# A kernel's head and tail: unit matrix and masks made on VectorE, GpSimd's first 64-bit addition put first, the last unit's halves interleaved

## The chip, the core and the metric

The kernel runs on one core of a Trainium2 chip. The time is device microseconds of one execution; the span is the time from the first to the last instruction of the profiled execution. The engines are called by their names in the profile: PE (TensorE), DVE (VectorE), ACT (ScalarE), POOL (GpSimd) and SP (SyncE, which issues DMAs).

## What is computed

Two attention blocks, A and B, each on its own x (2048 x 512), with 32 heads of 16 columns, and their outputs side by side in a 2048 x 1024 result, all in bfloat16:

```
qkv = (x @ wqkv) split into q, k, v, heads of 16
A (linear attention):  pq, pk = phi(q), phi(k);  phi(t) = t + 1 if t > 0 else exp(t), plus 1e-6
                       o = (pq @ (pk^T v)) / (pq . sum(pk) + 1e-6);  out = o @ wo
B (softmax attention): p = softmax(q k^T / 4);  o = p v;  out = o @ wo
```

## The kernel before

Block B is nearly all of the work. Its 32 heads are walked in 32 units: four groups of eight heads, in each four stretches of 512 queries, and in each of these an even and an odd half (four heads each, one per quarter of the PE array). A unit has 64 score blocks: 16 key tiles of 128 for each of the four heads. PE computes a block of scores (128 keys x 512 queries, line 916). Its exponential is taken in one of two ways. ACT does two or three blocks in one instruction (L1128), or DVE makes a 16-bit integer of the scores that, read as a 16-bit float, is nearly the exponential (L1032); POOL then makes two more copies of such a pair of blocks by adding a constant to four such integers at once, as one 64-bit addition (L1212, two additions for a group of two blocks). PE multiplies the results by the values (L1286) and gathers a unit's sums in one PSUM tile, pPV, in whose 32-row quarters 16 rows are sums and the 17th is the denominator. DVE transposes this tile in blocks of 32 x 32, takes reciprocals of the denominators, scales, and transposes back (L1315 to L1328; for the last unit L1378 to L1383, in two halves of 256 columns, so that the output product of the first half can begin before the second half is done). Block A's work (L623, L738 and others) fills gaps.

The order on each engine is fixed when the program is built. A planner holds a modelled clock for each engine and picks at each step among scores for ACT, scores for DVE, products with the values and small jobs. Its parameters change every 12 modelled us; they stand in the table SEG, one row per stretch. The 24th number of a row, DE3, says from which point on the last unit's groups no longer go to POOL: `late = left[NU - 1] < DE3 and ...`, with `left` the blocks of the last unit not yet taken. Where `late` holds, DVE makes the two copies itself (L1183). Jobs of the tail are put into lists (`urgent`, `urgent2`), each a sequence of steps with an engine and a modelled duration; the planner takes the first job of `urgent` as soon as it can start, and a job's next step when the one before is done.

Instructions wait for each other by semaphores. An instruction on an engine's queue that depends on an earlier one of the same queue also waits for it.

The head, before the planner begins, is written by hand:

- SP and ACT issue the loads: tiles 2 and 3 of x (ON), the first weights (Wb) by ACT; x transposed (xTb), the other weights and A's data by SP.
- DVE clears ZW, ZR and the tile pPV. POOL writes the iota FLG (one element, overwritten later by the flag that says whether scores are too large for this method), the unit matrix identb (`mk_ident`: clear, then select), the mask ZMk (`band`: which 16 rows belong to which of eight heads), clears EA and the start of DI, runs one 64-bit addition on zeros, and then writes the unit matrix identf, the mask BMk and the ones of VNa.
- DVE then reduces ZMk to PAR (even and odd heads' rows, L525), writes the ones of VV (L529, L531) and clears the second half of KM (L533).
- PE runs 30 products on ZW to warm up (L1401), transposes tiles 2 and 3 of x with identb (L1412), runs 8 more warming products, and makes the first keys and queries (L1424). DVE copies the one transposed tile (L609), ACT the other; DVE writes the masked keys KM with PAR (L1434). Then the first scores can be made (L916).

At the end every engine reads the flag (L1664) and jumps over a general softmax, which is in the program but not executed here (L1666), to two last instructions that the block's end adds (L372): a drain and a wait for all engines.

Of the kernel before, what the change touches and what calls it, by code (L numbers as in the profile page):

```python
# [8 lines left out]
F32 = mybir.dt.float32  # L9
# [3 lines left out]
ALU = mybir.AluOpType  # L13
# [225 lines left out]
def bass_concat_heads__linear_attn_block__softmax_full_mha__prompt_kernel(nc, A_x, A_wqkv, A_wo, B_x, B_wqkv, B_wo, out):  # L239
# [132 lines left out]
    with es:  # L372
# [44 lines left out]
        ZMk = sb("ZMk", [128, 8], F32)  # L417
        PAR = sb("PAR", [128, 2], F32)
# [82 lines left out]
        sch.add("pool", lambda e: e.iota(FLG.bitcast(mybir.dt.int32)[0:1, 0:1], [[0, 1]], base=0, channel_multiplier=0), writes=["FLG"])  # L501
        mk_ident(identb, "identb")
# [17 lines left out]
        band(ZMk, 8, 1, "ZMk")  # L520
        sch.add("pool", lambda e: e.memset(EA[:, 512:528], 0.0), writes=["EA"])
        sch.add("pool", lambda e: e.memset(DI[:, 0:64], 0.0), writes=[("DI", 0, 0, 0)])
        sch.add("pool", lambda e: e.int64_add(DW[:, 0:8], DW[:, 8:16], 0), reads=[("DI", 0, 0, 0)], writes=[("DI", 0, 0, 0)])
# [845 lines left out]
        def last_unit(u, t_):  # L1369

            Gp, c, e_ = unit(u)
            k, xb = 4 * Gp + c, (u // 2) % 2
            for h in range(2):
                cs = slice(256 * h, 256 * h + 256)
                o = PVb[:, cs].rearrange("p (m a r) -> p m a r", a=2, r=32)
                xn = XN[:, xb, cs].rearrange("p (m r a) -> p m a r", r=32, a=2)
                zr = ZR[:, 0, 8 * h:8 * h + 8].rearrange("p (m a) -> p m a", a=2)
                st = [("dve", 0.36, f_op("dve", lambda e, cs=cs: e.transpose(PVb[:, cs], PVb[:, cs]), [("PV", g) for g in range(4)], [("PVh", h)])),  # L1378
                      ("dve", 0.12, f_op("dve", lambda e, zr=zr, o=o: e.reciprocal(zr, o[:, :, :, 16]), [("PVh", h)], [("ZRh", h)] + [("ZR", 0)] * (h == 0))),
                      ("dve", 0.2, f_op("dve", lambda e, xn=xn, o=o, zr=zr: e.tensor_tensor(  # L1380
                          xn[:, :, :, 16 * e_:16 * e_ + 16], o[:, :, :, 0:16], zr.unsqueeze(3).broadcast_to([128, 4, 2, 16]), op=ALU.mult),
                          [("PVh", h), ("ZRh", h)], [("XNh", h)] + [("XN", xb, e_)] * (h == 0))),
                      ("dve", 0.2, f_op("dve", lambda e, cs=cs: e.transpose(on_at(k)[:, cs].bitcast(U32), XN[:, xb, cs].bitcast(U32)), [("XN", xb, 0), ("XNh", h)],  # L1383
                                        [("onh", h)] + (on_keys(k) if h == 0 else [])))]
                urgent.append(Job(st, [("zrh", 0)] if h else [("ot", u - 1)], [(1, ("zrh", h)), (3, ("onh", h))], bank=False, ready=t_, prio=-1))
                for tl in (2 * h, 2 * h + 1):
                    lane = "dve" if tl in (1, 3) else "act"
                    def last(bk, tl=tl):
                        tail_mm(tail["bk"][tl], tl, (3,))
                    def fin(bk, tl=tl, lane=lane):  # L1390
                        bk = tail["bk"][tl]
                        sch.add(lane, lambda e: copy_to(lane, lambda: obf(tl), lambda b: f32v(bk))(e, None), reads=[bk[3]], writes=kst(tl))
                        stores.append(sch.add(sch.new_dma_lane(), lambda e: e.dma_start(out[0][(12 + tl) * 128:(13 + tl) * 128, 512:1024], obf(tl)),
                                              reads=kst(tl), queue="act" if tl == 2 else "sp", force_signal=True))
                    urgent2.append(Job([("pe", 0.216, last), (lane, 0.6 if lane == "dve" else 0.52, fin)], [("onh", h), ("tail", tl)], [], bank=False))
# [324 lines left out]
```

## Time and profile before

| | us |
|---|---|
| runs | 657.56, 659.1, 660.05 (median 659.1) |
| profiled execution | 661.47 |
| its span | 660.0 |
| PE, ACT, DVE, POOL busy | 637.7, 632.5, 608.2, 430.0 |
| mean granted clock of PE | 0.994 |

The lines of a timeline read: start, length, engine, line of the kernel, operation, output <- input, shape, count, and in brackets the idle time before it with what ended it. "issue" there means that the engine waited for nothing that the profile shows. In waits, the columns are total, count and longest. Rows with a q behind the engine's name are of its instruction queue (branches, drains, semaphores, DMA issues), which don't count as busy. The line numbers are those of the kernel before.

### The profile page before, as it was taken

What the parts mean: (1) busy time and instruction counts of PE and PEld (TensorE: products, weight loads), DVE (VectorE), ACT (ScalarE), POOL (GpSimd) and SP (SyncE); (2) the same over time, 40 slices, a digit from 0 to 9 for tenths busy, and PEclk for the clock granted to TensorE, in tenths of its full rate; (3) what the DMA queues carried; (4) which work ended last, traced back from release to release, by engine and by line L of the source; (5) the groups of instructions that cost most, each with busy time, mean ns of one, the idle gap of its engine ahead of it and who ended that gap; (6) DMA issues with size and microseconds to landing.
All of it is one profiled execution on the core that took longest, in us unless ns stands there. A gap on an engine that the chain in (4) does not pass through costs nothing.

```text
span 660.0 us, 19615 instructions
## 1 busy us (share of the span) xinstructions
PE 637.7 (97%) x8365; PEld 215.1 (33%) x8366; DVE 608.2 (92%) x1078; ACT 632.5 (96%) x688; POOL 430.0 (65%) x733
## 2 busy tenths in 40 slices
PE   5999999999999999999999999999999999999994
PEld 4434333334333433333333232323222232232221
DVE  3799999999999998999999999999999999988983
ACT  1999999999999999999999999999999999999993
POOL 0367776777876766677767667666777766656550
PEclk9999999999999999999999999999899999999998
DMA  9700010011001000102121111002100001101111
GB/s 218 166 2 2 10 34 13 7 40 20 19 2 33 2 10 5 39 8 44 34 66 33 33 26 27 17 9 51 41 9 18 1 18 42 33 10 35 53 46 44
DMA packets 53229, 21.77 MB, mean 33 GB/s; under 512 B 44176, under 2 KB 52624, under 8 KB 53136
## 3 DMA queue, kind: packets, MB, share of 16 engines
q1 hardware_dynamic: 51664, 19.80, 13.0%
q8 instruction: 67, 1.10, 0.7%
q10 hardware_dynamic: 1472, 0.66, 0.4%
q14 instruction: 26, 0.21, 0.1%
HBM read 4.46 MB, written 4.19 MB: 13 GB/s over the span
## 4 chain that ended last, share of the span: by engine, by line
PE 49%; ACT 40%; DVE 8%; issue 2%; DMA 1%; POOL 0%; DVEq 0%; POOLq 0%
ACT PT L1128 38%; PE pPV L1286 18%; PE pS L916 17%; PE pD L623 6%; DVE DI L1032 4%; PE pS L623 3%; PE pD L722 1%; ACT EA L738 1%; PE pD L916 1%; PE pS L722 1%; DMA KNa<-VNa 1%; DVE pPV L1315 1%; PE pS L679 1%; DVE KNa L609 0%; DVE VNa L828 0%
## 5 line engine op out<-in xcount | busy, mean ns | idle before, releaser
L1128 ACT ACTIVATE PT<-pS 128x1024 f16<-128x1024 f32 (+1 forms) x650 | 619.4, 1102 | 6.6 <-PE pS L916 5.4
L1212 POOL INT64_ADD DI<-DI x714 | 427.0, 611 | 197.5 <-DVE DI L1032 195.4
L1032 DVE TENSOR_SCALAR DI<-pD 128x512 int16<-128x512 f32 x499 | 329.4, 683 | 19.0 <-PE pD L916 14.2
L916 PE MATMUL pS<-QT,KM 32*128 32x512 bf16 x1547 | 263.3, 386 | 3.4 <-ACT PT L1128 2.6
L1286 PE MATMUL pPV<-PT,VV 128*17 128x512 f16 x1333 | 236.3, 381 | 0.0
L1286 PE MATMUL pPV<-DI,VV 128*17 128x512 f16 x1430 | 228.2, 381 | 0.0
L916 PE MATMUL pD<-QT,KM 32*128 32x512 bf16 x501 | 175.5, 385 | 0.4 <-DVE VNa L828 0.2
L1286 PE MATMUL pPV<-DI,VX 128*17 128x512 f16 x715 | 163.9, 382 | 0.3 <-DVE OT L1320 0.2
L1032 DVE TENSOR_SCALAR DI<-pS 128x512 int16<-128x512 f32 x214 | 145.3, 679 | 1.6 <-PE pS L916 1.4
L916 PEld LDWEIGHTS pS<-QT,KM 32*128 32x128 bf16 x1547 | 66.9, 91 | 238.0 <-ACT PT L1128 188.3
L1286 PEld LDWEIGHTS pPV<-PT,VV 128*17 128x17 bf16 x1333 | 52.3, 88 | 45.3 <-issue 36.8
L1286 PEld LDWEIGHTS pPV<-DI,VV 128*17 128x17 bf16 x1430 | 51.6, 88 | 42.7 <-issue 27.8
L916 PEld LDWEIGHTS pD<-QT,KM 32*128 32x128 bf16 x501 | 42.0, 91 | 4.0 <-DVE DI L1032 1.5
L1286 PEld LDWEIGHTS pPV<-DI,VX 128*17 128x17 bf16 x715 | 36.3, 89 | 21.3 <-issue 14.2
L623 PE MATMUL pD<-Wa,xTa 128*32 128x256 bf16 x704 | 28.6, 275 | 0.4 <-DVE DI L1032 0.4
L623 PE MATMUL pD<-xTb,Wb 128*32 128x512 bf16 x336 | 27.8, 396 | 0.0
L1315 DVE STREAM_TRANSPOSE pPV<-pPV 128x512 f32<-128x512 f32 x31 | 22.4, 722 | 0.0
L623 PEld LDWEIGHTS pD<-Wa,xTa 128*32 128x32 bf16 x704 | 14.9, 95 | 10.9 <-issue 6.6
L623 PE MATMUL pD<-xTa,Wa 128*32 128x512 bf16 x192 | 15.7, 384 | 0.3 <-DVE DI L1032 0.2
L738 ACT ACTIVATE EA<-pD 128x512 bf16<-128x512 f32 x24 | 15.8, 657 | 0.0
L623 PE MATMUL pD<-Wa,KNa 128*32 128x512 bf16 x176 | 14.8, 406 | 0.9 <-DMA KNa<-VNa 0.7
L1320 DVE TENSOR_TENSOR OT<-pPV,ZR 128x256 bf16<-128x256 f32 x31 | 13.9, 447 | 1.1
(137 smaller groups left out, 343.4 us busy)
## 6 DMA issues: line engine op xcount, KB each, us to landing
out_dram<-KNa SPq DMA_DIRECT2D x31, 128.0 KB, 1.7
Wa<-in_A_wqkv_dram SPq DMA_DIRECT2D x1, 1536.0 KB, 8.4
KM<-KR SPq DMA_DIRECT2D x96, 16.0 KB, 1.8
Wb<-in_B_wqkv_dram SPq DMA_DIRECT2D x2, 384.0 KB, 5.3
Wb<-in_B_wqkv_dram SPq DMA_DIRECT2D x1, 512.0 KB, 4.5
Wa<-in_A_wo_dram SPq DMA_DIRECT2D x1, 512.0 KB, 4.2
Wa<-in_B_wo_dram SPq DMA_DIRECT2D x1, 512.0 KB, 3.7
ON<-in_B_x_dram ACTq DMA_DIRECT2D x1, 256.0 KB, 3.0
```

Source lines behind the costliest of these rows:

```text
L623: ins = self.e.matmul(out_[32 * g:32 * g + 32], lhsT=lhsT[:, 32 * g:32 * g + 32], rhs=rhs, start=start, stop=stop, tile_position=(0, 32 * g))
L679: return e.matmul(f32v(bk)[:, tl * 128:(tl + 1) * 128], lhsT=xTb[:, cc, t * 128:(t + 1) * 128], rhs=xTb[:, cc, t * 128:(t + 1) * 128], sta ...
L722: return e.matmul(f32v(bk)[:, tl * 128:(tl + 1) * 128], lhsT=xTb[:, cc, t * 128:(t + 1) * 128], rhs=Wb[:, cc, 1024 + Gp * 128:1024 + Gp * ...
L738: ("act", 0.0635 + n * 0.000833, f_ev("act", lambda e, bk: e.activation(EA[:, 0:n], f32v(bk)[:, c0:c0 + n], ACTF.Exp), [], ["EA"])),
L916: return e.matmul(dst, lhsT=KM[32 * g:32 * g + 32, Gp % 2, e_, j * 128:(j + 1) * 128], rhs=QT[32 * g:32 * g + 32, Gp % 2, c * 512:(c + 1) ...
L1032: sch.add("dve", lambda e: e.tensor_scalar(DI[:, di_at(0, buf) + i * 512:di_at(0, buf) + (i + n) * 512], f32v(DBANK[b0], n * 512), ESC, EB ...
L1128: sch.add("act", lambda e: e.activation(PTf[:, p0 * 512:p0 * 512 + w], S5[:, c0:c0 + w], ACTF.Exp, scale=SC), reads=skeys(sl, len(bl)), wr ...
L1212: sch.add("pool", lambda e, v=v, word=word: e.int64_add(at64(v), at64(0), word), reads=keys, writes=[("DI", v, x) for x in best])
L1286: sch.add("pe", lambda e, g=g, j=j, c0=c0, V_=V_, r2=r2, P=P, first=first, last_=last_: e.matmul(PVb[32 * g:32 * g + 17, 0:512], lhsT=V_[: ...
L1315: sch.add("dve", lambda e: e.transpose(PVb[:, 0:512], PVb[:, 0:512]), reads=[("PV", g) for g in range(4)], writes=[("PV", g) for g in rang ...
L1320: sch.add("dve", lambda e: e.tensor_tensor(xn[:, :, :, 16 * e_:16 * e_ + 16], o[:, :, :, 0:16], zr.unsqueeze(3).broadcast_to([128, 8, 2, 1 ...
```

## The change

Three parts.

First, the head. The iota on FLG is gone. POOL begins with the clearing of DI and its one 64-bit addition. DVE makes identb and ZMk: it writes 0 to 127 along the columns of identf by doubling (a column of zeros, then seven additions that copy the columns so far, plus 1, 2, 4 to 64), transposes the first 32 columns in blocks of 32 x 32 into IC, so that each quarter has its row number modulo 32 in column 0, adds 32, 64 and 96 to the quarters, and compares identf with that column; the result is the unit matrix identb. ZMk is the maximum over groups of 16 columns of it. POOL still writes identf (over DVE's row of numbers), BMk and VNa's ones, after DVE's compare.

Second, DE3 is 0 in all rows of SEG, so the last unit's groups all go to POOL.

Third, the last unit's two halves are one job of eight DVE steps, in which each step is done for both halves before the next.

```
-        (48.0,0.1,4,3,0,1,6,4,9.0,28,3.0,6.0,1.8,1.8,2,5.0,2.0,3,1.0,2,1,1.0,8,14,-0.1,4,0,2),
+        (48.0,0.1,4,3,0,1,6,4,9.0,28,3.0,6.0,1.8,1.8,2,5.0,2.0,3,1.0,2,1,1.0,8,0,-0.1,4,0,2),
...
-        (636.0,0.3,4,3,0,1,6,4,10.0,26,2.5,7.0,0.5,1.8,2,5.0,2.0,3,1.0,2,1,1.0,6,14,-9.0,4,0,82),
+        (636.0,0.3,4,3,0,1,6,4,10.0,26,2.5,7.0,0.5,1.8,2,5.0,2.0,3,1.0,2,1,1.0,6,0,-9.0,4,0,82),
...
+        IC = sb("IC", [128, 32], F32)
...
         sch.add("dve", lambda e: e.memset(ZW[:], 0.0), writes=["ZW"])
-        sch.add("pool", lambda e: e.iota(FLG.bitcast(mybir.dt.int32)[0:1, 0:1], [[0, 1]], base=0, channel_multiplier=0), writes=["FLG"])
-        mk_ident(identb, "identb")
+        sch.add("pool", lambda e: e.memset(DI[:, 0:64], 0.0), writes=[("DI", 0, 0, 0)])
+        sch.add("pool", lambda e: e.int64_add(DW[:, 0:8], DW[:, 8:16], 0), reads=[("DI", 0, 0, 0)], writes=[("DI", 0, 0, 0)])
+        sch.add("dve", lambda e: e.memset(identf[:, 0:1], 0.0), writes=["identf"])
+        for k_ in (1, 2, 4, 8, 16, 32, 64):
+            sch.add("dve", lambda e, k_=k_: e.tensor_scalar(identf[:, k_:2 * k_], identf[:, 0:k_], float(k_), None, op0=ALU.add), reads=["identf"], writes=["identf"])
+            if k_ == 16:
+                sch.add("dve", lambda e: e.transpose(IC[:], identf[:, 0:32]), reads=["identf"], writes=["IC"])
+        for q_ in range(1, 4):
+            sch.add("dve", lambda e, q_=q_: e.tensor_scalar(IC[32 * q_:32 * q_ + 32, 0:1], IC[32 * q_:32 * q_ + 32, 0:1], 32.0 * q_, None, op0=ALU.add), reads=["IC"], writes=["IC"])
+        sch.add("dve", lambda e: e.tensor_scalar(identb[:], identf[:], IC[:, 0:1], None, op0=ALU.is_equal), reads=["IC", "identf"], writes=["identb"])
+        sch.add("dve", lambda e: e.tensor_reduce(ZMk[:], identb[:].rearrange("p (a b) -> p a b", b=16), axis=AX.X, op=ALU.max), reads=["identb"], writes=["ZMk"])
         sch.add("dve", lambda e: e.memset(DUM, 0.0), writes=[("ZR", 0)])
...
-        band(ZMk, 8, 1, "ZMk")
         sch.add("pool", lambda e: e.memset(EA[:, 512:528], 0.0), writes=["EA"])
-        sch.add("pool", lambda e: e.memset(DI[:, 0:64], 0.0), writes=[("DI", 0, 0, 0)])
-        sch.add("pool", lambda e: e.int64_add(DW[:, 0:8], DW[:, 8:16], 0), reads=[("DI", 0, 0, 0)], writes=[("DI", 0, 0, 0)])
...
+            def t1(h):
+                cs = slice(256 * h, 256 * h + 256)
+                return f_op("dve", lambda e: e.transpose(PVb[:, cs], PVb[:, cs]), pv_, [("PVh", h)])
...
+            steps = [("dve", 0.28, t1(0)), ("dve", 0.33, t1(1)), ("dve", 0.25, rc(0)), ("dve", 0.2, rc(1)), ("dve", 0.2, sc_(0)), ("dve", 0.2, sc_(1)), ("dve", 0.24, t2(0)), ("dve", 0.24, t2(1))]
+            urgent.append(Job(steps, [("ot", u - 1)], [(6, ("onh", 0)), (7, ("onh", 1))], bank=False, ready=t_, prio=-1))
             for h in range(2):
-                cs = slice(256 * h, 256 * h + 256)
...
-                urgent.append(Job(st, [("zrh", 0)] if h else [("ot", u - 1)], [(1, ("zrh", h)), (3, ("onh", h))], bank=False, ready=t_, prio=-1))
```

What this does to the order, at three places. First, the start of DVE's order; ZW, ZR and pPV are cleared tiles, ZMk and PAR the masks. Before:

```order
L500 MEMSET ZW 128x64
L503 MEMSET ZR 1x8
L505 MEMSET pPV 128x512
L525 TENSOR_REDUCE PAR<-ZMk 128x1 x2
L529 MEMSET VV 128x132
```

and what stands between ZW and ZR now:

```order
L504 MEMSET identf 128x1
L506 TENSOR_SCALAR identf<-identf 128x1
L506 TENSOR_SCALAR identf<-identf 128x2
L506 TENSOR_SCALAR identf<-identf 128x4
L506 TENSOR_SCALAR identf<-identf 128x8
L506 TENSOR_SCALAR identf<-identf 128x16
L508 STREAM_TRANSPOSE IC<-identf 128x32
L506 TENSOR_SCALAR identf<-identf 128x32
L506 TENSOR_SCALAR identf<-identf 128x64
L510 TENSOR_SCALAR IC<-IC 32x1 x3
L511 TENSOR_SCALAR identb<-identf,IC 128x128
L512 TENSOR_REDUCE ZMk<-identb 128x8
```

These fourteen instructions stand between ZW and ZR now; ZR, pPV, PAR and what follows are as they were.

Second, POOL's start, where "ISA DI<-DI" is the 64-bit addition and the bare ISA before it an instruction that configures the engine. Before:

```order
L501 ISA
L501 IOTA FLG 1x1
L496 MEMSET identb 128x128
L497 AFFINE_SELECT identb<-identb 128x128
L515 MEMSET ZMk 128x8
L516 AFFINE_SELECT ZMk<-ZMk 128x8
L518 AFFINE_SELECT ZMk<-ZMk 128x8
L521 MEMSET EA 128x16
L522 MEMSET DI 128x64
L523 ISA
L523 ISA DI<-DI 128x16
L496 MEMSET identf 128x128
```

and now:

```order
L502 MEMSET DI 128x64
L503 ISA
L503 ISA DI<-DI 128x16
L530 MEMSET EA 128x16
L497 MEMSET identf 128x128
```

One of the two configurations is gone with the iota, and the other stands near the front.

Third, DVE's end, with the last group's shifts (L1183) and the last unit. Before:

```order
L1032 TENSOR_SCALAR DI<-pD 128x512 x4
L1183 TENSOR_SCALAR DI<-DI 128x1024 x2
L609 CAST KNa<-pD 128x512
L1378 STREAM_TRANSPOSE pPV<-pPV 128x256
L1379 RECIPROCAL ZR<-pPV 128x8
L1380 TENSOR_TENSOR OT<-pPV,ZR 128x4x2x16
L1383 STREAM_TRANSPOSE xTb<-OT 128x128
L1378 STREAM_TRANSPOSE pPV<-pPV 128x256
```

and now:

```order
L1039 TENSOR_SCALAR DI<-pD 128x512 x4
L616 CAST KNa<-pD 128x512
L1386 STREAM_TRANSPOSE pPV<-pPV 128x256 x2
L1389 RECIPROCAL ZR<-pPV 128x8 x2
L1392 TENSOR_TENSOR OT<-pPV,ZR 128x4x2x16 x2
L1396 STREAM_TRANSPOSE xTb<-OT 128x128 x2
```

The two shifts are the last two 64-bit additions of POOL now (210 stand in its last row where 208 stood). The orders of PE, ACT and SP are the same as before, and DVE's and POOL's between these places too.

More of the change, by code (lines that the diff above doesn't have):

```diff
@@ L1372, in last_unit @@
             k, xb = 4 * Gp + c, (u // 2) % 2
-            for h in range(2):
-                cs = slice(256 * h, 256 * h + 256)
[L1375 to L1384, printed above, removed]
-                urgent.append(Job(st, [("zrh", 0)] if h else [("ot", u - 1)], [(1, ("zrh", h)), (3, ("onh", h))], bank=False, ready=t_, prio=-1))
@@ new lines, in last_unit, with rc @@
+            o = PVb[:, 0:512].rearrange("p (m a r) -> p m a r", a=2, r=32)
+            xn = XN[:, xb, :].rearrange("p (m r a) -> p m a r", r=32, a=2)
+            zr = ZR[:, 0, 0:16].rearrange("p (m a) -> p m a", a=2)
+            pv_ = [("PV", g) for g in range(4)]
+            def t1(h):
+                cs = slice(256 * h, 256 * h + 256)
+                return f_op("dve", lambda e: e.transpose(PVb[:, cs], PVb[:, cs]), pv_, [("PVh", h)])
+            def rc(h):
+                m = slice(4 * h, 4 * h + 4)
+                return f_op("dve", lambda e: e.reciprocal(zr[:, m, :], o[:, m, :, 16]), [("PVh", h)], [("ZRh", h)] + [("ZR", 0)] * (h == 0))
@@ new lines, in sc_, with t2 @@
+            def sc_(h):
+                m = slice(4 * h, 4 * h + 4)
+                return f_op("dve", lambda e: e.tensor_tensor(xn[:, m, :, 16 * e_:16 * e_ + 16], o[:, m, :, 0:16], zr[:, m, :].unsqueeze(3).broadcast_to([128, 4, 2, 16]), op=ALU.mult),
+                            [("PVh", h), ("ZRh", h)], [("XNh", h)] + [("XN", xb, e_)] * (h == 0))
+            def t2(h):
+                cs = slice(256 * h, 256 * h + 256)
+                return f_op("dve", lambda e: e.transpose(on_at(k)[:, cs].bitcast(U32), XN[:, xb, cs].bitcast(U32)), [("XN", xb, 0), ("XNh", h)], [("onh", h)] + (on_keys(k) if h == 0 else []))
```

50 rows, old and new, of the table SEG are left out of this document.

## The prediction

> **What bounds the kernel now.** I read the chain of waits first, then the busy time in windows, then the timelines of the first 25 and the last 20 us, because the change touches nothing else. The chain is shared by TensorE and ScalarE, and in the middle both are busy all the time:
>
> ```profile
> PE 49%; ACT 40%; DVE 8%; issue 2%; DMA 1%; POOL 0%; DVEq 0%; POOLq 0%
> ...
> 30.00:100.00 70.00, 69.98 (x946) 24.11 (x938) 67.95 (x120) 70.00 (x77) 50.44 (x85) 1.00 0.05 12
> 474.20:477.60 3.40, 3.40 (x29) 0.73 (x30) 2.87 (x6) 2.67 (x4) 1.58 (x4) 0.50 0.22 43
> ```
>
> The windows' columns are the stretch, its length, the busy time of PE, PEld, DVE, ACT and POOL, the granted clock, DMA share and GB/s. From 30 to 100 us PE is busy for 69.98 and ACT for 70.00 of 70 us. The instructions of both stay in the same order, so whatever moves their start moves the whole middle with it, and the end too. The start is where time is lost, as the waits of the first 20 us say:
>
> ```profile
> DVE PAR L525 <- POOL ZMk L518: 8.4, 1, 8.4
> POOL FLG L501 <- issue: 8.2, 1, 8.2
> POOL DI L523 <- issue: 6.8, 1, 6.8
> ```
>
> GpSimd stands 8.2 us before its iota and 6.8 us before its first 64-bit addition, each time for nothing that the profile shows. VectorE waits 8.4 us for the mask ZMk behind the first of these. The timeline shows what hangs on it:
>
> ```profile
> 0.94 0.07 DVE L503 MEMSET ZR<- 1x8 f32 x1
> 1.06 3.38 PE L1401 MATMUL pD<-ZW 128*128 128x128 bf16 x30 [1.06 <-DVE ZR L503]
> 1.11 0.48 DVE L505 MEMSET pPV<- 128x512 f32 x1
> 9.46 1.03 PE L1412 MATMUL pS<-identb,ON 128*128 128x128 bf16 x8 [5.02 <-POOL ZMk L515]
> 10.02 0.22 DVE L525 TENSOR_REDUCE PAR<-ZMk 128x1 f32<-128x4 f32 x2 [8.43 <-POOL ZMk L518]
> 10.65 0.17 DVE L529 MEMSET VV<- 128x132 bf16 x1 [0.41 <-issue]
> 13.88 0.36 DVE L609 COPY xTb<-pS 128x512 bf16<-128x512 bf16 x1
> 14.39 1.01 PE L1424 MATMUL pS<-xTb,Wb 128*128 128x256 bf16 x4 [1.76 <-DVE xTb L609]
> 16.61 1.03 PE L916 MATMUL pS<-QT,KM 32*128 32x512 bf16 x5
> 17.57 1.90 PE L623 MATMUL pD<-xTb,Wb 128*32 128x512 bf16 x16
> 19.93 0.74 PE L722 MATMUL pD<-Wb,xTb 128*128 128x128 bf16 x8
> 20.05 12.88 ACT L1128 ACTIVATE PT<-pS 128x1536 f16<-128x1536 f32 x13 [0.42 <-PE pS L916]
> 23.20 0.83 PE L623 MATMUL pD<-xTb,Wb 128*32 128x512 bf16 x12
> ```
>
> Two chains leave GpSimd. One is identb, then the transposes on PE at 9.46. The other, the longer, is ZMk, PAR on VectorE at 10.02, 3.86 us of memsets, then the copy of x's tile at 13.88, the query product at 14.39 and the first scores at 16.61. VectorE works in order, so the copy cannot pass the memsets.
>
> **The head.** GpSimd loses the iota, identb and ZMk; VectorE gets 14 small instructions ahead of ZR and PV. Their count: a column memset, seven doublings, a transpose, three column additions, a compare, a reduction. No such chain stands in the trace. The nearest rows are a pair of small dependent VectorE instructions, and one of the compare's shape:
>
> ```profile
> 212.09 0.18 DVE L695 TENSOR_TENSOR GRW<-GRW,ZMk 128x32 f32<-128x32 f32 x1
> 212.30 0.19 DVE L697 TENSOR_REDUCE TOP<-GRW 128x1 f32<-128x32 f32 x1
> ...
> L815 DVE TENSOR_SCALAR RD<-pD 128x128 f32<-128x128 f32 x4 | 1.1, 282 | 0.6 <-PE pD L812 0.6
> ```
>
> From 212.09 to 212.30 is 0.21 us for one step. I take: column memset 0.17 (as from ZR at 0.94 to PV at 1.11), ten doublings and additions at 0.205 = 2.05, the compare 0.3 (282 ns and a gap), the transpose and the reduction 0.3 each (more than the 0.19 of a 32-wide reduction, no more than the 128-wide transpose's 0.31 below), then ZR 0.05 and PV 0.49. That is 3.66 us from 0.94, so PAR starts at 4.6 instead of 10.02: **5.4 us** earlier. Bounds: if a small step takes only 0.11, half of the 0.22 of PAR's two, the sum is 2.7 and the gain 6.4; if each of the 13 dependent steps has a pause like the 0.41 before L529, the sum is 5.3 + 0.6 and the gain 3.1. I take 5.4, since the pair of dependent rows is the nearest kin.
>
> Does the 5.4 arrive at the scores? Other arrivals must be earlier than the new times:
>
> ```profile
> Wb<-in_B_wqkv_dram SPq DMA_DIRECT2D x1, 512.0 KB, 4.5
> ON<-in_B_x_dram ACTq DMA_DIRECT2D x1, 256.0 KB, 3.0
> Wb<-in_B_wqkv_dram ACTq DMA_DIRECT2D x2, 128.0 KB, 4.3
> xTb<-in_B_x_dram SPq DMA_TRANSPOSE x4, 5.4
> ```
>
> These are the DMA issues of the first 20 us, the last column from issue to landing. x's tiles (ON, issued at 0.8) are there at 3.8, identb at about 3.8, and PE's 30 warming products end at 4.44: the transposes run from 4.5 to 5.5, well before the copy at 8.5. The first weights and xTb are there at about 6.6, when the eight further warming products end. The next load (512 KB, issued at 5.7) lands at 10.2 and is wanted 3.3 us after the first scores (19.93 now), so at about 14.5: DMA becomes the bound only for a gain above 9 us. GpSimd's one remaining stall, 6.8 to 8.2 us from 0.9, ends by 9.1; identf, BMk and VNa (1.9 us) follow, and its first shift can be due only after the first scores near 11 us and VectorE's 0.68 on them: that work is hidden.
>
> **The cold start of PE.** At 17.57 sixteen projections take 1.90 us, at 23.20 twelve take 0.83, or 1.11 for sixteen: until about 20 us PE works at half pace, though the granted clock shown there is 1.00. In the changed kernel PE has work from 1.06 to about 8.0 nearly without a pause, where now it idles 5.02 us, so the fast pace can come before the first scores. Worth at most 0.5 (half of the 1.01 at 14.39) plus the 0.42 that ACT idles at 20.05, and nothing if the pace comes as late after the start as now. I take **0.6**, range 0 to 0.9; what the projections gain lies beside ACT's exponentials. [...]
>
> **The tail.** Now the rows where the last unit is normalised, and those of the last group of shifts:
>
> ```profile
> 642.21 1.20 POOL L1212 INT64_ADD DI<-DI  x2 [0.76 <-DVE DI L1032]
> 642.71 1.29 DVE L1032 TENSOR_SCALAR DI<-pD 128x512 int16<-128x512 f32 x2 [0.60 <-PE pD L916]
> 644.03 0.76 DVE L1183 TENSOR_SCALAR DI<-DI 128x1024 int16<-128x1024 int16 x2
> 647.13 0.39 PE L1286 MATMUL pPV<-DI,VV 128*17 128x512 f16 x2
> 648.95 0.47 DVE L1378 STREAM_TRANSPOSE pPV<-pPV 128x256 f32<-128x256 f32 x1 [3.56 <-PE pPV L1286]
> 650.03 0.31 DVE L1383 STREAM_TRANSPOSE xTb<-OT 128x128 uint32<-128x128 uint32 x1
> 651.30 0.31 DVE L1383 STREAM_TRANSPOSE xTb<-OT 128x128 uint32<-128x128 uint32 x1
> 651.54 0.65 DVE L609 CAST KNa<-pD 128x512 bf16<-128x512 f32 x1
> 652.31 0.69 DVE L609 CAST KNa<-pS 128x512 bf16<-128x512 f32 x1
> ```
>
> The two VectorE shifts (L1183, 0.76) go to GpSimd: it is free from 643.4, can start 0.17 after 644.0 and needs 1.2, so 645.4, and PE wants them from 646.9 on. I cost that at nothing; without the 1.5 us of cover each further us would delay the last products one for one. Each half now takes four dependent steps, 1.39 us, one half behind the other: 648.95 to 650.34 and to 651.61. Interleaved, each step runs in the shadow of the other half's: eight starts 0.25 to 0.38 apart (a start-to-start of 0.24 stands between the independent pair at 650.03 and 650.27) put the first half's end at about 650.7 and the second's at about 651.0. The first pair of products is 0.4 later, the second 0.6 earlier. The end is the second CAST, which follows the first at 0.65 to 0.77; the first now waits for VectorE's last transpose and will wait for PE instead, at about 651.4, so the second ends near 652.7 instead of 653.0: **0.3**, between a loss of 0.4 (if the first half's path decides) and a gain of 0.65.
>
> **The end.** At the end every engine jumps over the code for large scores to two last instructions. The rows of these two, and the instruction transfers of the page:
>
> ```profile
> L372 DVEq DRAIN  x1: 57/57/57, 656.8 to 656.8; - x1
> L372 PEldq EVENT_SEMAPHORE  x1: 51/51/51, 657.1 to 657.1; - x1
> L372 DVEq EVENT_SEMAPHORE  x1: 21/21/21, 660.0 to 660.0; - x1
> ...
> q8 instruction: 67, 1.10, 0.7%
> q14 instruction: 26, 0.21, 0.1%
> ```
>
> All others are done at 657.1, VectorE alone at 660.0: its last instruction comes 3.2 us after the one before it. PE's 16,731 instructions came in 67 packets of 16.4 KB, 66 bytes each; the other queue's packets are 8.1 KB, thus about 125 instructions. I read the 2.9 us as a border of such a packet that falls just between VectorE's last two instructions. The change puts 14 instructions ahead and takes 2 away: the stream is 12 longer, the border lies 12 earlier against its end, and both last instructions come with one packet. Worth **2.9**, or nothing if the reading is wrong. [...]
>
> **The sum.** 5.4 + 0.6 + 0.3 + 2.9 = 9.2 us. The profiled execution took 661.47 with a span of 660.0, which becomes 652.3; the median of the three runs is 659.1, which becomes 649.9. I say **650.0**.
>
> **The rivals.** *The end's stall stays* (it belongs to the jump, not to a border): 659.1 - 6.3 = 652.8. For it: from VectorE's last CAST, over at 653.0, to its DRAIN at 656.8 the jump alone already costs 3.8; against it: no other engine has a second stall. *VectorE's chain is dear*, 0.4 us a step as before L529: gain 3.1 in the head and none in pace, 659.1 - 3.1 - 0.3 - 2.9 = 652.8, and 655.7 if the end's stall stays as well. *The gain is given back in the middle*, by a wait on something whose time doesn't move: 659.1 - 0.3 - 2.9 = 656 to 659. The loads landing by 10.2 and the full PE and ACT speak against it. *The change doesn't do what it says*: by the order it does, with the exception that two shifts move though the order is called as it was. [...]
>
> **How the numbers follow.** Forecast 0.58; stall stays 0.20; dear chain 0.12; given back 0.07; slower 0.03. The likeliest gives 650.0. Its own range is 647.5 to 652; low end of all: 6.4 + 0.9 + 0.65 + 2.9 = 10.9 gives 648.2, less the 1.5 by which the lowest run lies under the median, 646.7. High end: 652.8 and the same spread, 654.5. So 646.7 to 654.5. What this kernel's measurement can tell from no change is about 0.5%, 3.3 us: faster, below 655.8, 0.90; within 0.07; slower 0.03.
>
> **What would show it.** Right: GpSimd has one stall of 6 to 8 us and nobody waits behind it; PAR at 4 to 5; the first scores at 10.5 to 11.3 and the first exponential half a us behind; in the middle every instruction about 6 us earlier; VectorE's last instruction within 0.4 us of the others. Wrong: PAR after 6; a DMA named as releaser in the first 15 us; PE waiting for GpSimd's DI in the last 5 us; VectorE alone at the end again.

## The result, and the profile after

The changed kernel took 651.32 us (median of 4 runs, 650.58 to 653.45) against 659.58 (657.56 to 662.01) beside it: a ratio of 0.9879, 95% interval 0.9836 to 0.9921. In a second set, taken later, it took 649.78 (5 runs) against 659.9 (11 runs): 0.9852, interval 0.9831 to 0.9874. The forecast was 650.0, in a range of 646.7 to 654.5. The profiled execution has a span of 648.7 us where before's had 660.0, so 11.3 us less; the medians differ by 8.3 and 10.1. That the two profiled executions are further apart than the forecast's sum of 9.2 has to be explained as well.

The timeline of the changed kernel's head (start, duration, engine, line, operation, what it writes and reads). Lines 502 to 512 are the new head; behind it a line number is 7 higher than before, at the end up to 14.

```profile
0.80 0.15 POOL L502 MEMSET DI<- 128x64 int16 x1 [0.29 <-POOLq L1719]
1.06 0.98 DVE L506 TENSOR_SCALAR identf<-identf 128x1 f32<-128x1 f32 x5
1.09 0.20 POOL L503 INT64_ADD DI<-DI  x1
...
3.60 0.29 DVE L512 TENSOR_REDUCE ZMk<-identb 128x8 f32<-128x128 bf16 x1
...
4.41 0.15 DVE L532 TENSOR_REDUCE PAR<-ZMk 128x1 f32<-128x4 f32 x2
...
8.19 0.36 DVE L616 COPY xTb<-pS 128x512 bf16<-128x512 bf16 x1
...
8.70 0.60 PE L1438 MATMUL pS<-xTb,Wb 128*128 128x256 bf16 x4 [1.46 <-DVE xTb L616]
...
9.89 0.60 PE L923 MATMUL pS<-QT,KM 32*128 32x512 bf16 x5
...
12.16 0.62 PE L729 MATMUL pD<-Wb,xTb 128*128 128x128 bf16 x8
...
17.05 0.39 PE L1293 MATMUL pPV<-PT,VV 128*17 128x512 f16 x4
```

Five doublings take 0.98 us, PAR starts at 4.41 instead of 10.02 (5.61 earlier), x's copy at 8.19 instead of 13.88 (5.69), the first scores at 9.89 instead of 16.61 (6.72), the first products with values (L1293) at 17.05. Their row in before, from the same view:

```profile
24.51 0.39 PE L1286 MATMUL pPV<-PT,VV 128*17 128x512 f16 x4
```

So from there on the changed kernel is 7.46 us ahead: 1.85 more than PAR gained. GpSimd shows neither of its two stalls. Its first 64-bit addition starts 0.29 us behind the memset before it, and its longest wait in the first 25 us is for VectorE's first scores:

```profile
POOL DI L1219 <- DVE DI L1039: 15.5, 3, 12.9
```

The columns are the total, the number of waits and the longest. The middle is as full as before (windows: PE, PEld, DVE, ACT and POOL busy, then the granted clock), and one half-clock window is there again:

```profile
23.00:93.00 70.00, 69.98 (x945) 24.36 (x946) 67.94 (x119) 70.00 (x77) 49.99 (x84) 1.00 0.11 32
467.70:471.10 3.40, 3.40 (x29) 0.65 (x30) 2.51 (x6) 2.51 (x3) 2.02 (x4) 0.50 0.17 50
```

The last unit and the end, from the timeline and from the rows of the last two instructions (duration min/median/max in ns, first and last start):

```profile
641.38 0.80 DVE L1386 STREAM_TRANSPOSE pPV<-pPV 128x256 f32<-128x256 f32 x2 [3.71 <-PE pPV L1293]
...
642.70 0.49 DVE L1396 STREAM_TRANSPOSE xTb<-OT 128x128 uint32<-128x128 uint32 x2
...
643.70 0.69 DVE L616 CAST KNa<-pD 128x512 bf16<-128x512 f32 x1 [0.51 <-PE pD L1347]
...
644.30 0.68 DVE L616 CAST KNa<-pS 128x512 bf16<-128x512 f32 x1
```

```profile
L372 DVEq EVENT_SEMAPHORE  x1: 21/21/21, 648.7 to 648.7; - x1
L372 PEldq EVENT_SEMAPHORE  x1: 51/51/51, 648.7 to 648.7; - x1
...
L372 DVEq DRAIN  x1: 57/57/57, 648.4 to 648.4; - x1
```

From the first transpose (641.38; before 648.95, so 7.57 earlier) to the end of the last CAST it takes 3.60 us instead of 4.05. VectorE's last instruction comes 0.3 behind its DRAIN, and with the others. The 11.3 us of the span are thus 7.5 won before the middle (5.6 by the earlier PAR and 1.85 by PE's pace, as the experiments show), 0.45 of tail, 2.9 of end, and 0.4 that the step from the last CAST to the other engines' last instruction became shorter (4.1 to 3.7), which I did not follow up.

### The profile page after: what moved, and what is told of

The parts are those of the page before. It is cut to its first block, busy times and chain, and to the rows that moved or that the text cites. A ratio compares the mean times of both kernels' runs of the same rounds, so it can differ in the third digit from the quotient of the medians.

```text
span 648.7 us, 19621 instructions
## 1 busy us (share of the span) xinstructions
PE 634.6 (98%) x8366; PEld 214.4 (33%) x8366; DVE 608.7 (94%) x1090; ACT 632.1 (97%) x688; POOL 430.3 (66%) x729
## 4 chain that ended last, share of the span: by engine, by line
PE 49%; ACT 41%; DVE 8%; DMA 1%; issue 1%; DVEq 0%
ACT PT L1135 40%; PE pPV L1293 19%; PE pS L923 17%; PE pD L630 5%; DVE DI L1039 4%; PE pS L630 3%; ACT EA L745 1%; PE pD L729 1%; PE pD L923 1%; PE pS L729 1%; DMA KNa<-VNa 1%; DVE pPV L1322 1%; PE pS L686 1%; DVE KNa L616 0%; DVE VNa L835 0%
## 5 line engine op out<-in xcount | busy, mean ns | idle before, releaser
L1293 PE MATMUL pPV<-PT,VV 128*17 128x512 f16 x1333 | 236.6, 381 | 0.0
L1293 PE MATMUL pPV<-DI,VV 128*17 128x512 f16 x1430 | 228.7, 382 | 0.0
L1293 PE MATMUL pPV<-DI,VX 128*17 128x512 f16 x715 | 164.0, 383 | 0.3 <-DVE OT L1327 0.3
L1293 PEld LDWEIGHTS pPV<-PT,VV 128*17 128x17 bf16 x1333 | 52.4, 88 | 45.3 <-issue 36.9
L1293 PEld LDWEIGHTS pPV<-DI,VV 128*17 128x17 bf16 x1430 | 51.7, 88 | 42.8 <-issue 27.9
L1293 PEld LDWEIGHTS pPV<-DI,VX 128*17 128x17 bf16 x715 | 36.3, 89 | 21.5 <-issue 14.5
L616 DVE CAST KNa<-pD 128x512 bf16<-128x512 f32 x20 | 13.6, 682 | 2.3 <-PE pD L630 1.8
```

Source lines behind the costliest of these rows:

```text
L616: return lambda e, bk: (e.tensor_copy(out_fn(), in_fn(bk)) if lane == "dve" else e.activation(out_fn(), in_fn(bk), ACTF.Copy))
L1293: sch.add("pe", lambda e, g=g, j=j, c0=c0, V_=V_, r2=r2, P=P, first=first, last_=last_: e.matmul(PVb[32 * g:32 * g + 17, 0:512], lhsT=V_[: ...
```

## The experiments

The blocks with - and + give each edit in short, mostly in words. A stream is all instructions of an engine in the built program, those of the general softmax, which is not executed, included.

**The head alone.** The head of the change, with before's sequential halves and its two shifts on VectorE.

```diff
-        iota FLG, identb and ZMk on pool; first int64_add behind them
+        int64_add first on pool; identf/IC/identb/ZMk chain on dve
         (last unit and table of shifts as before)
```

> The head of the change alone; the tail and the two last shifts stay as before. VectorE's stream is 14 longer than before. Theory (the terms add up: head about 7.5 us, end 2.9, tail 0.45): the middle runs 7.5 us earlier than before, as with the whole change; from the first transpose of the last unit to the end of VectorE's last CAST it takes 4.05 us as before (3.60 with the whole change); VectorE ends with the others; span 0.45 us above the whole change's 648.7, about 649.2, time 651 to 652.5. Rival (the gain of the tail and of the moved shifts is larger than the 0.45 read from the trace, or a part of the head's gain hangs on them): span 650.5 or more.

Measured: 651.85 us (5 runs, 651.39 to 652.75), ratio 0.9866, 0.9846 to 0.9886; profiled span 650.9, median span 650.1 against 649.6 for the change's first four runs. The last unit takes 4.05 us again and VectorE ends with the others. But the middle is 6.21 us ahead (first products with values at 18.30), not 7.5, though VectorE's rows are those of the change. The windows say why:

```profile
4.80:8.20 3.40, 1.70 (x21) 1.13 (x19) 2.65 (x13) 0.98 (x2) 0.57 (x3) 1.00 1.06 185
8.20:11.60 3.40, 2.90 (x17) 1.57 (x17) 2.47 (x9) 0.02 (x1) 0.00 (x0) 0.50 1.12 294
11.60:15.00 3.40, 3.08 (x38) 1.42 (x37) 1.74 (x4) 3.40 (x3) 0.00 (x0) 1.00 1.06 183
```

Here the full clock came at 4.8, PE was busy for 1.70 of the next 3.40 us (it waits for the copy), and the window after that ran at 0.50, which cost 1.25 us. The change has the same head, and neither of its two profiled executions has such a window, so this is not the edit's. The pace at the start is not a constant of the program: from 8.2 to 11.6 us the granted clock was 0.50 here and 1.00 in the change. The profiled span is 1.7 us above the expected 649.2, which is what the rival had named; 1.25 of it are this window, and the other 0.4 lie behind the last CAST, which ends 4.1 us before the others' last instruction, as in before. The median span, 650.1, is below the rival's bound. A larger share for the tail is not needed, though single spans don't settle a few tenths.

**The tail alone.** Interleaved halves and moved shifts on before's head. VectorE's stream has 3264 instructions instead of 3266.

```diff
-        two Jobs of four steps, one per half; VectorE may take the last shifts
+        one Job of eight steps, halves alternating; shifts all on GpSimd
         (head as before)
```

> The interleaved halves of the last unit and the moved shifts alone; the head stays as before. VectorE's stream is 2 shorter than before. Theory (a border of an instruction packet between VectorE's last two instructions made the stall, so a shift of the border by 2 in either direction removes it): VectorE's last instruction within 0.4 us of the others', span 2.9 + 0.45 = 3.3 us below before's, time about 0.5% below before. Rival (the stall belongs to the jump at the end, or the head took it away): VectorE's last instruction still 2.9 us behind the others, span 0.4 below before's.

Measured: 658.74 us (12 runs) against 660.14 (23 runs), ratio 0.9979, 0.9962 to 0.9996. VectorE ends with the others:

```profile
L372 DVEq EVENT_SEMAPHORE  x1: 21/21/21, 654.0 to 654.0; - x1
L372 PEldq EVENT_SEMAPHORE  x1: 51/51/51, 654.0 to 654.0; - x1
```

So the head is not what removed the stall, and the jump is not what makes it. Yet the time fell by 1.4 us only, while the median span fell from 658.7 to 655.3: what lies outside the span grew from 1.44 to 3.39 us. The trace has an instruction packet at 656.78, 2.8 us behind the last recorded instruction. I read this as the border lying just behind the stream's end now, with the fetch waited for there, outside the span; the time outside the span fits (3.01 to 3.84 us in all 12 executions, 1.38 to 1.53 in the 23 of before), the wait itself is not in the trace.

**One memset more.** Before, with one more small memset on VectorE where it waits for ZMk.

```diff
         memset PVb
+        sch.add("dve", lambda e: e.memset(PVb[:, 0:1], 0.0), ...)
```

> Before with one more memset of one column (about 0.06 us) on VectorE, put where it waits 8.4 us for ZMk, so it costs nothing there. VectorE's stream is 1 longer. Theory (packet border): the border now falls ahead of both last instructions, they come in one packet, VectorE's last instruction within 0.4 us of the others', span 2.9 us below before's 660.0, every time up to the last store as before. Rival (jump, or anything of the work itself): VectorE's last instruction 2.9 us behind the others as before, same span.

```profile
L372 DVEq EVENT_SEMAPHORE  x1: 21/21/21, 655.3 to 655.3; - x1
L372 PEldq EVENT_SEMAPHORE  x1: 51/51/51, 655.3 to 655.3; - x1
```

The stall is gone: 658.30 us (12 runs), ratio 0.9965, 0.9948 to 0.9982. In the medians that is 1.84, where the span's 2.9 less 0.3 (1.44 outside it become 1.75) would give 2.6, inside the interval (1.2 to 3.4). What I had not expected: the span is 4.6 us shorter, not 2.9. "Every time as before" does not hold, although nothing ahead of the end was changed. Rows of the timeline, to be held against 16.61 (1.03 for five) and 24.51 of before:

```profile
15.52 0.60 PE L917 MATMUL pS<-QT,KM 32*128 32x512 bf16 x5
...
22.67 0.39 PE L1287 MATMUL pPV<-PT,VV 128*17 128x512 f16 x4
```

The same head, 1.84 us ahead. The trace's first record of a full granted clock is at 20.23 us in before and at 12.64 here (ahead of a first record the windows show 1.00 too, though in before the five products at 16.61 took 1.03 us, against 0.60 here at 15.52). The half-clock records of these traces, those behind the last product aside, last 3.41 us each (467.7 to 471.1 above). Counting windows of 3.41 us back from these two points, first before, then this kernel (the second number is PE's busy time):

```profile
9.99:13.40 3.41, 2.64 (x21) 2.03 (x19) 2.40 (x12) 0.98 (x2) 0.12 (x2) 1.00 1.12 233
13.40:16.82 3.42, 2.43 (x16) 1.57 (x17) 2.49 (x10) 0.00 (x0) 0.00 (x0) 1.00 1.15 270
16.82:20.23 3.41, 3.41 (x28) 0.86 (x24) 1.48 (x4) 2.55 (x3) 1.67 (x7) 1.00 0.98 185
```

```profile
9.23:12.64 3.41, 3.17 (x24) 2.56 (x24) 1.70 (x10) 0.63 (x2) 0.69 (x6) 1.00 1.13 275
```

Counted so, before's windows with 2.64 and 2.43 us busy had no full clock behind them and the one with 3.41 had; here, with the count shifted by 0.76 us, one window holds 3.17, and the full clock stands behind it, 7.6 us earlier. That such windows decide is my reading of these rows; that the two starts differ is measured. The other kernels' traces fit: the last window ahead of the full clock has PE busy for 2.92 us or more, and none before it for more than 2.64. The tail-alone kernel, with the same head, has it at 12.80 and its values' products at 22.75. So 1.85 us of the 11.3 were the luck of before's profiled execution, a late one.

**No iota.** Before without the iota and with the 64-bit addition first; identb and ZMk stay on GpSimd, VectorE gets no chain.

```diff
-        pool: iota FLG; identb; ZMk; memset DI; int64_add
+        pool: memset DI; int64_add; identb; ZMk
```

> Before with the iota taken out and the first 64-bit addition put first on GpSimd; identb and ZMk stay on GpSimd, VectorE has none of the new chain. VectorE's stream is as long as before. Theory (GpSimd's two stalls of 8.2 and 6.8 us belong to the iota: one to load what the iota needs and one to load what the addition needs, which is there from the start): no stall on GpSimd, ZMk done at about 2.7 (0.2 to 0.35 us an operation), PAR at about 3, about 1.4 us earlier than with the change; PAR to first scores as in the change, 5.5 us or less, so first scores at 8.5 to 9.5 unless the loads hold them; the middle 7.5 to 9 us earlier than before; VectorE's last instruction 2.9 us behind the others as before. Span 651 to 652.5. Rival (the first library operation of GpSimd pays 6 to 8 us whichever it is, and the change escaped it only because nobody waited): GpSimd stalls 6 to 8 us ahead of the addition, ZMk at 9 or later, span within 2 us of before.

Measured: 652.66 us (5 runs), ratio 0.9885, 0.9863 to 0.9906, with before's tail and before's stall at the end. Rows of its head and its end:

```profile
1.09 0.20 POOL L502 INT64_ADD DI<-DI  x1
...
2.27 0.19 POOL L519 TENSOR_SCALAR_AFFINE_SELECT ZMk<-ZMk 128x8 f32<-128x8 f32 x1
...
2.50 0.22 DVE L524 TENSOR_REDUCE PAR<-ZMk 128x1 f32<-128x4 f32 x2 [0.90 <-POOL ZMk L519]
...
8.24 0.60 PE L915 MATMUL pS<-QT,KM 32*128 32x512 bf16 x5
...
16.38 0.39 PE L1285 MATMUL pPV<-PT,VV 128*17 128x512 f16 x4
```

```profile
L372 PEldq EVENT_SEMAPHORE  x1: 51/51/51, 648.9 to 648.9; - x1
L372 DVEq EVENT_SEMAPHORE  x1: 21/21/21, 651.2 to 651.2; - x1
```

Two operations moved and one taken out give the whole gain of the head and 0.7 us more (16.38 against 17.05). The two stalls belonged to the iota: without it the masks cost GpSimd 1.2 us, and VectorE need not make them. That something is loaded in the stalls, as the theory has it, no trace shows. With 3266 instructions VectorE is 2.3 us late at the end again.

**The change with the iota put back** as GpSimd's first operation.

```diff
+        pool: iota FLG
         pool: memset DI; int64_add
```

> The whole change with the iota put back as GpSimd's first operation, ahead of the addition; nothing reads what it writes in the head. Theory (the stalls of 8.2 and 6.8 us belong to the iota, which needs something loaded that the addition does not, and the addition then needs its own loaded again): GpSimd stalls about 8 us from 0.9 and about 7 us before the addition, both for nothing that the profile shows; its head work ends at about 20 instead of 5.4, so its first shift, at 18.4 with the change, comes 1 to 2 us later; VectorE's PAR stays at 4.4 and the first scores at 9.9; time within 2 us of the change's 651.3. Rival (the addition pays for its load whatever stands ahead; with the change it was free by some chance): one stall or none.

The waits of GpSimd in its first 40 us:

```profile
POOL DI L1220 <- DVE DI L1040: 9.4, 8, 2.6
POOL FLG L502 <- issue: 8.2, 1, 8.2
POOL DI L504 <- issue: 5.9, 1, 5.9
```

Both stalls are back, 8.2 and 5.9 us, and nobody waits for them: head work done at 16.8, the first shift at 19.41 behind VectorE, 652.25 us (4 runs, ratio 0.9875, 0.9849 to 0.9902), not told apart from the change. The first scores came at 10.73, not at 9.9, and the first products with values at 18.11, but behind VectorE's copy at 8.19 as in the change: as with the head alone, PE was busy for only 1.62 us of a full-clock window, and the next, from 8.93 to 12.34, ran at half clock. The estimate of 20 for the end of the head work was 3 us too late. So either half of the change's head would have done: no iota, or nothing that waits for GpSimd.

**The border brought back.** The change with VectorE's clears moved to GpSimd and one reduction saved: 3267 instructions; and with the memset of ZR moved as well: 3266.

```diff
-        dve: 4 memsets VV, 8 memsets KM, 2 reductions PAR
+        pool: 4 memsets VV, 8 memsets KM; dve: 1 reduction PAR   (3267)
-        dve: memset ZR
+        pool: memset ZR                                          (3266)
```

> The whole change with VectorE's twelve clears of VV and KM, its memset of ZR and one of its two PAR reductions taken off it (the first two to GpSimd, the reductions made one): VectorE's stream has 3266 instructions again, as before the change. Theory (packet border between the last two instructions when their count is 3266): VectorE's last instruction 2.3 to 2.9 us behind the others although the end of the program is the change's own. In the head the copy of x's tile comes at about 5.5 to 6.5 instead of 8.19, the first scores near 8.3, and from there on the 512 KB load, which lands at 10.4 to 10.6, holds the values' products, so the middle is 0.5 to 0.8 us earlier than with the change at the same start of the full clock. Span about 2 us above the change's. Rival (border is not the cause): VectorE's last instruction within 0.4 us of the others, span 0.5 to 0.8 below.

> The same with the memset of ZR left on VectorE: 3267 instructions, one more. Theory (border): VectorE's last instruction with the others, 2.3 to 2.9 us less at the end than in the kernel with 3266, which differs by this one memset of 0.07 us; time 0.3 to 1 us below the change's where the start of the full clock is the same. Rival: both kernels end alike.

With 3266:

```profile
L372 PEldq EVENT_SEMAPHORE  x1: 51/51/51, 647.9 to 647.9; - x1
L372 DVEq EVENT_SEMAPHORE  x1: 21/21/21, 650.4 to 650.4; - x1
```

With 3267:

```profile
L372 DVEq EVENT_SEMAPHORE  x1: 21/21/21, 649.9 to 649.9; - x1
L372 PEldq EVENT_SEMAPHORE  x1: 51/51/51, 649.9 to 649.9; - x1
```

651.88 us (0.9886, 0.9864 to 0.9909) and 650.10 (0.9854, 0.9821 to 0.9886), 6 runs each: one memset of 0.07 us makes 2.5 us of stall. Stream lengths of 3267, 3278 and 3280 have no stall, 3266 has it in three kernels with different heads, and with 3264 about as much time lies outside the span. That the place of VectorE's last instructions in its stream makes the stall is shown. That the engine waits for a packet there is a reading: the last instruction packet comes 2.6 to 3.2 us behind the one before it in the four kernels with 3266 or 3264 (at 660.68 in before, 0.7 us behind VectorE's last instruction), and at most 0.6 us behind it in the ten others, but the trace doesn't say which engine a packet is for.

The head did not come out as expected: x's copy is at 6.8, not 5.5 to 6.5, since VectorE's chain became slower. The first scores are at 8.79 with 3266 and at 10.84 with 3267, the first products with values at 16.08 and 18.00; the full clock begins at 4.94 in the one profiled execution and at 10.38 in the other, so the medians, 1.8 us apart, hold more than the stall. The doublings (groups by line, with the mean in ns behind the busy time) with 3267 instructions, then in the change itself:

```profile
L506 DVE TENSOR_SCALAR identf<-identf 128x1 f32<-128x1 f32 (+6 forms) x7 | 3.4, 487 | 0.3
```

```profile
L506 DVE TENSOR_SCALAR identf<-identf 128x1 f32<-128x1 f32 (+6 forms) x7 | 1.2, 174 | 0.3
```

Beside twelve memsets on GpSimd a doubling takes 487 instead of 174 ns in the mean: 154 in both for the one of one column, which is over before these memsets begin, 216 to 769 for the others. The three additions in one column stay at 146 in both.

**Fewer and more warming products.** The change once more, with 2 instead of 30 products at the start, and with 12 more in PE's pause before the copy.

```diff
-    WARM = (30, 8)
+    WARM = (2, 8)                          (fewer)
+        warm(12)                           (more)
         first_mm(q1, 0, 2, 2, 0)
```

> The change itself, for the three beside it on the same chip. Theory (the full clock of PE begins at a window border whose place differs from execution to execution, by up to about 2 us of the span): spans between 648 and 652, median time 650.5 to 652.5, the middle 5.6 to 7.5 us earlier than in the profiled execution of before, by where the full clock begins.

> The change with 2 instead of 30 warming products at the start: PE has nothing to do from 1.3 us to the transposes at 4.2. Theory (a window of 3.41 us counts towards the full clock only if PE was busy through it): the first window that is busy enough ends later, the full clock never begins before 8.5 us, first scores at 10.3 to 10.8 instead of 9.89, median span 0.5 to 1.5 us above the change's. Rival (the clock does not hang on the warming products): the same spans as the change's.

> The change with 12 further warming products between the first eight products of the queries and keys and those that wait for VectorE's copy, where PE idles from 7.2 to 8.7 us; they end before the copy at either clock (0.7 or 1.4 us). Theory (a window with this gap in it falls back to half clock, as in the run of the head alone from 8.20 to 11.61, and costs 1.2 us): no half-clock window between 5 and 25 us, spans all within 1.2 us of the lowest, median span 0.3 to 0.8 below the change's. Rival (the gap is too short to matter, only the phase of the windows does): spans spread as the change's do, over 3 us.

The change: 649.78 us (spans 647.5 to 650.9), a little below what was expected. With 2 products: 653.78 (6 runs, ratio 0.9893, 0.9873 to 0.9912; spans 649.9 to 653.2); with 12 more: 650.50 (5 runs, 646.9 to 650.8). In the profiled execution with 2 products the full clock begins at 12.84, and the first scores and a later window read:

```profile
10.91 1.03 PE L923 MATMUL pS<-QT,KM 32*128 32x512 bf16 x5
```

```profile
309.80:313.20 3.40, 3.40 (x46) 1.12 (x38) 3.19 (x7) 2.91 (x4) 1.90 (x4) 0.50 0.02 5
```

With the 28 products the first scores came 1.0 us earlier and the first values 1.24, and the full clock began at 6.92 in the change instead of 12.84. With the starts of one head 7.6 us apart, one profiled execution with 2 products doesn't settle that the clock hangs on them. That a window counts only if PE was busy through it is not borne out: by the count above, 3.17 of 3.41 us were enough with one memset more. The medians are 4.0 us apart, though, where 0.5 to 1.5 were expected: in the profiled executions (spans of 653.2 and 648.0) two half-clock windows add about 1.3 us each to those 1.24; the rest, and why its other executions are slow too, are not shown. Filling the pause gained nothing: the values' products are at 17.04 as against 17.05, because VectorE's memsets set the copy, at 8.19 in both, and the four products behind it take 0.60 us, the full clock's time, in both.

The spans still spread over 3.9 us (3.4 in the change's), for a reason that I had not on the list: half-clock windows deep in the program, at 309.8 here, 308.3 with 12 more products, 309.3 with the iota put back, and near 470. ACT's instructions show about 1.3 us lost in each, and the profiled execution of the change's second set has neither. All executions say the same by their mean granted clock: the nine of the change have spans of 647.5 to 648.8 us at 0.996 to 0.999 and of 650.3 to 651.7 at 0.991 to 0.994. What makes a window fall to half pace is open. PE's busy time alone doesn't: in the kernel with one memset more a window with 1.72 us busy was followed by full clock, and in before one with 2.55 by the half-clock window at 474.2:

```profile
12.64:16.05 3.41, 1.72 (x18) 1.13 (x18) 3.13 (x12) 0.45 (x2) 0.00 (x0) 1.00 0.97 197
```

```profile
470.80:474.20 3.40, 2.55 (x21) 0.82 (x17) 3.40 (x7) 3.40 (x4) 2.79 (x5) 1.00 0.00 0
```

**A version without VectorE's chain.** The change with identb and ZMk on GpSimd behind the addition, and three small memsets so that VectorE has 3267 instructions.

```diff
-        dve: identf, IC, identb, ZMk (14 instructions)
+        pool: identb, ZMk behind int64_add; dve: 3 memsets of one column
```

> The whole change without VectorE's new chain: identb and ZMk stay on GpSimd, behind the 64-bit addition that now comes first, and the iota is gone; three small memsets bring VectorE's stream to 3267. Theory (what the change gains in its head is the iota's two stalls, and VectorE's chain is not needed for it): PAR at 2.5 instead of 4.41, first scores at 8.2 instead of 9.89, the 512 KB load then holds, so the middle is 0.7 us earlier than with the change at the same start of the full clock; VectorE ends with the others; time 650 to 652, not more than 1 us from the change's. Rival (VectorE's chain is what gains): PAR after 4.4, middle later than with the change.

> The kernel with identb and ZMk on GpSimd behind the addition once more, beside the change on one chip. Expected 0.7 us below the change at the same clock, 0.3 to 2 us in the medians.

```profile
2.50 0.22 DVE L527 TENSOR_REDUCE PAR<-ZMk 128x1 f32<-128x4 f32 x2 [0.50 <-POOL ZMk L522]
...
8.13 0.60 PE L918 MATMUL pS<-QT,KM 32*128 32x512 bf16 x5
...
15.83 0.39 PE L1288 MATMUL pPV<-PT,VV 128*17 128x512 f16 x4
```

649.67 us (6 runs, 0.9843, 0.9819 to 0.9868) and 650.64 (4 runs, 0.9861, 0.9842 to 0.9881). By the trace its head is 1.1 to 1.2 us ahead of the change's (15.83 and 15.94 against 17.05). In the times the two are not told apart: in the set where both ran, where this kernel was expected 0.3 to 2 lower, the change was 0.9 lower; between the other two sets the change was 1.7 higher. It is simpler and not slower; that it beats the change by more than its spread is not shown.

## Why the prediction was right, and where not

- **The head, 5.4**: right, 5.6 measured. The step of 0.205 fits (five doublings in 0.98), PAR came at 4.41 instead of 4.6. It arrived in full: from the execution of before's head with a full clock (values at 22.67) to the change's (17.05) are 5.62. No DMA became the releaser of anything that set the scores.
- **PE's cold start, 0.6, range 0 to 0.9**: this step failed. The profiled executions differ by 1.85 through the pace, twice the upper bound, but by the luck of before's, which a memset cannot have changed. As a fixed term it is not told from nothing; as a spread it is 1.25 us one way (the head alone) and 1.85 the other. The earlier pace also put the first scores at 9.89, ahead of the 10.5 to 11.3 named as the sign of being right: the full clock began at 6.92 and the stretch from x's copy to the scores took 1.70 us instead of 2.73. The term had to be a spread of both signs: between two executions of one head the start of the full clock moved by 7.6 us (20.23 in before, 12.64 with one memset more).
- **The tail, 0.3**: right, mis-sized by 0.15: 4.05 became 3.60.
- **The end, 2.9**: right in place, and in the span. Of the cause, that the place in the stream decides is shown, by the five stream lengths above; the waiting for a packet is a reading, and so is the share of PE in the 67 packets, an estimate from the page's counts and bytes, since the trace doesn't say which engine a packet is for. 0.3 us are given back outside the span, so 2.6. The rival that the stall belongs to the jump is out.
- **The shifts at nothing**: nothing to see of them. The last unit begins 7.57 us earlier, as much as the middle gained and 0.1 more.
- **GpSimd keeps one stall of 6 to 8 us**: wrong. I took it that one stall would stay, whichever operation came first; with the iota there are two (8.2 and 6.8 us in before, 8.2 and 5.9 with it put back), without it none. Nobody waited there, so it cost the sum nothing, but it hid the better reading: the waits list named the iota, and GpSimd's masks were late only because they stood behind it.
- **The sum**: 5.6 + 0.45 + 2.6 = 8.65 us against medians of 8.3 and 10.1. The 9.2 was near for the medians and 2 short for the two profiled executions, by the 1.85 of the clock. The high end of the range has a slip: 652.8 and the same spread of 1.5 is 654.3, not 654.5. The forecast of 650.0 leaned on a term that was no term, and on luck of about 1 us. The rival of a dear chain fell with the doublings' 0.2 us, that of a gain given back with the 7.46 that stays to the end. As for slower, at 0.03: half-clock windows were in the runs, at about 1.3 us each, but a profiled execution has none to three of them, too few to use up 8.3 us of gain.

## What to carry to other kernels

Where an engine waits for a first operation, ask which earlier instruction made it stall; taking that one away can be worth as much as moving the work, and costs less: here the first products with values came at 16.38 us without the iota and at 17.05 with the work moved. Before a gap between two profiled executions is put down to an edit, compare the row at which PE's pace changes: here one memset "gained" 1.84 us at a place it could not touch. And look at the last two instructions of each engine: one that ends alone, some us behind its own DRAIN, may be cured by a single instruction more or less, if the time outside the span is watched too: here one memset brought 3.2 us down to 0.6 inside the span, and 0.3 came back outside it.

## What had not been expected of the hardware

- GpSimd's iota cost a stall of 8.2 us, and the 64-bit addition behind it 5.9 to 6.8; with the addition first and no iota there is none, and the five memsets and selects of identb and ZMk take 1.2 us.
- The start of PE's full clock differed by 7.6 us between two executions of one head (12.64 and 20.23), worth 1.84 us to the end.
- With a stream of 3264 instructions, two fewer than before, the time outside the span was 3.39 us instead of 1.44 to 1.78.
- Deep in the program the pace of PE fell to half for 3.41 us at one or two places (near 309 and 470) in some executions of one kernel and in others not, at about 1.3 us each.
- VectorE's doublings took 487 instead of 174 ns in the mean while GpSimd ran memsets; single-column additions, at 146 ns, were not slowed. Why those two differ was not tried.
